# Relu-squared attention and a GELU feed-forward block on one core: what the first load gate of batch 2 reads

## The chip, the cores and the metric

The kernel runs on one core of a Trainium2 chip. The metric is the device time of one execution in microseconds (us). TensorE (PE) multiplies matrices, ScalarE (ACT) and VectorE (DVE) do the elementwise work and empty the PSUM memory that the PE writes to, GpSimd (POOL) and SyncE (SP) do almost nothing here but issue DMAs. A DMA issued by POOL and one issued by SP run on the same 16 DMA engines; the profile calls POOL's queue q0 (software_dynamic) and SP's q1 (hardware_dynamic).

## The reference

Eight batches of twelve heads, 448 tokens, head size 64. The attention has no softmax: the scaled scores go through relu and are squared. Its output, 3584 rows of 768, goes through two matrix products with an exact GELU in between.

```python
def _attn_ref(q, k, v):
    S = q.shape[2]
    scale = 1.0 / np.sqrt(q.shape[-1])
    scores = scale * np.matmul(q, k.transpose(0, 1, 3, 2))
    attn = np.maximum(scores, 0.0) ** 2 / S
    return np.matmul(attn, v)

def _moe_ref(x, w_in, w_out):          # x: 3584 x 768, w_in: 768 x 2048, w_out: 2048 x 768
    h = x @ w_in
    g = 0.5 * h * (1.0 + erf(h / sqrt(2)))
    return g @ w_out
```

## The kernel before

**Batches and groups.** A batch's twelve heads are taken as three groups of four (G = 3). Work is written as operations with an engine, a function and dependencies; a long string, ORDER, then fixes by hand the order in which each engine gets them. Every engine works its own list in order, so an instruction that waits holds up all that stands behind it on that engine. The dependencies listed with an operation serve the ordering alone; the waits in the program come from what each instruction reads and writes.

**Loads.** POOL issues all loads of q, k, v and the weights (L463, L552, L570, L480 to L482, L486). They convert float32 in HBM to bf16 in SBUF on the way. The output weights come in three parts (`add_wout`): part 1 is two DMAs of 384 KB, part 0 one DMA of 1536 KB, part 2 again two of 384 KB.

**Transposes.** For batches 0 and 1 the PE transposes q and k. From batch 2 on SP does it by DMA (`add_T_dma`): for each group a transpose of k into kT (L666), one of q into a segment of the tile qT (L666, called "even" below), and then two plain copies within qT that swap the upper and lower 64 partitions into the next segment (L686 and L687, called "the swap"). Segment 2g of qT holds the transposed q of group g, segment 2g + 1 its exchanged copy. In SP's list for batch 2 the order is: q of group 0, k of group 0, q of group 1, swap of group 0, k of group 1, swap of group 1, q of group 2, swap of group 2, k of group 2. A swap reads what a transpose writes, so SP waits for that transpose to land before it issues the swap. The transposes and copies of one batch and group are called q0, k0, swap 0, q1, k1, swap 1 and so on below.

**Gates.** A gate (`add_gate`, L709) is a copy of 128 x 16 elements on POOL whose result nobody uses. It reads from a segment of qT and so makes POOL wait until the DMA that writes this segment has landed; the loads behind it in POOL's list go out only then. There are three gates for each of the batches 2 to 6. For batch 2 all three read the exchanged copy (segment 2g + 1), for later batches the transposed q itself (segment 2g).

POOL's list around batch 2 is: gate of group 0; output weights part 1; gate of group 1; k of group 2 of batch 2; output weights part 0; v of group 0 of batch 2; q of groups 0 and 1 of batch 3; output weights part 2; gate of group 2; v of group 1 of batch 2, k of groups 0 and 1 of batch 3, and so on.

**Who uses what.** On the PE the scores of batch 2 (L741) need kT and both segments of the group: group 0 from the first scores on, group 1 from the third run of scores on (the fifth product of the twelve that start together at 58.94 us in the profile). They are put between products of the feed-forward block (L854, h = x @ w_in). The products with w_out that need the output weights first are at L1267 (`add_plain`, part 0 alone for the first two), followed by Strassen-like products (L1172, L998).

```python
        for g in range(G):
            op = turn(k_dst(g), k_src(g), list(ld_k[b, g]))
            ...
            even = turn(q_dst(g), q_src(g), lands)
            both = sch.add(
                (("SP", SWAP_STEP, SWAP_TIME),), swapped(g), [even] + after.pop(0), mode="X"
            )
            for c in range(NC):
                Tq[b, g, c] = (even, both)
```

Of the kernel before, what the change touches and what calls it, by code (L numbers as in the profile page):

```python
# [24 lines left out]
SEG = 4 * NC // 2 * KC  # L25
# [373 lines left out]
def kernel(  # L399
# [9 lines left out]
    nc = tc.nc  # L409
# [81 lines left out]
    def get_T(b):  # L491
        if b not in qkT:
            qkT[b] = (
                tpool.tile([128, QCOLS], BF16, tag="qT", name="qT"),
                tpool.tile([128, G, NK * 128], BF16, tag="kT", name="kT"),
            )
        return qkT[b]
# [5 lines left out]
    def q_seg(b, n):  # L503

        return get_T(b)[0][:, SEG * n : SEG * n + SEG]
# [31 lines left out]
    Tq, Tk = {}, {}  # L537
# [165 lines left out]
    gate = const.tile([128, 16], BF16, tag="gate", name="gate")  # L703

    def add_gate(b, g):


        def fn(e):
            nc.gpsimd.tensor_copy(gate, q_seg(b, 2 * g + (b == 2))[:, : SEG : SEG // 16])  # L709

        deps = [Tq[b, g, 0][b == 2], Tk[b, g, 0][0]]
        pool_q.append(sch.add((("POOL", 0.2, 0.3),), fn, deps))

    xT, hT = {}, {}
# [682 lines left out]
    add_steps(steps(1), ATT1_BIAS, True)  # L1397
    add_T_dma(2, [[]] * 9)
    add_gate(2, 0)
    add_wout(0)  # L1400
    add_wout(1)
    add_gate(2, 1)
    add_wout(2)
    add_gate(2, 2)
    for m in range(0, HALF_M, 2):
        add_f1(0, m, 1, bias=F1B_BIAS)
# [135 lines left out]
```

## Time and profile before

| what | value |
|---|---|
| time, median of 3 runs | 371.41 us (370.39 to 371.74) |
| the profiled execution's own time | 370.35 us |
| its span, first to last instruction | 368.2 us |
| PE busy | 358.2 us (97%) |
| DVE busy | 287.9 us (78%) |
| ACT busy | 192.0 us (52%) |
| POOL busy (issuing loads included) | 62.7 us (17%) |
| granted TensorE clock, mean | 0.998 |
| the first gate of batch 2 starts | 52.07 us |

The span is what the engines' instructions cover; the execution's own time is 2.15 us longer. All positions in the text are in us from the start of the span. A row of the timeline gives start, duration, engine, line, operation and tiles, and in brackets the idle time before it with what ended it; of an engine called SPq it is the issuing of a DMA, not its transfer. The DMA view of a narrow window lists the DMAs issued in it with the time from issue to landing.

### The profile page before, as it was taken

To read this page: it belongs to the slowest core of one execution; us is meant where nothing else is said; L and a number is where in the kernel's file an instruction comes from. 1 tells how busy PE (TensorE), PEld (TensorE's weight loads), DVE (VectorE), ACT (ScalarE), POOL (GpSimd) and SP (SyncE) were. 2 spreads that over 40 slices of the span, in tenths; PEclk is the share of its full clock that TensorE was granted. 3 is DMA by queue.
4 is the path that set the end of the run, shared out by engine and by line. 5 is a ranking of instruction groups with operands and counts; after the bars stand their busy time and mean duration, and the time that the engine had idled before them with its cause. 6 is when DMAs were issued, how large, how long until landed. Compare 5 with 4: busy or idle time off the path is not lost.

```text
span 368.2 us, 8480 instructions
## 1 busy us (share of the span) xinstructions
PE 358.2 (97%) x3560; PEld 222.2 (60%) x3560; DVE 287.9 (78%) x480; ACT 192.0 (52%) x312; POOL 62.7 (17%) x101
## 2 busy tenths in 40 slices
PE   8799999999899999999999999999999999999995
PEld 7576654445444555544555544477888787867663
DVE  4999863479886899898669999999977866667753
ACT  5998867626267553768666366860514134232200
POOL 8576116130050060050401000000000000000000
PEclk9999999999999999999999999999999999999999
DMA  9999999999999999999999960000300202022233
GB/s 170 199 199 199 200 154 122 203 183 177 229 179 216 181 167 187 248 180 190 156 175 178 194 129 2 2 2 0 88 2 0 88 25 62 2 85 87 85 85 88
DMA packets 75046, 47.10 MB, mean 128 GB/s; under 512 B 38528, under 2 KB 71552, under 8 KB 75008
## 3 DMA queue, kind: packets, MB, share of 16 engines
q0 software_dynamic: 32912, 22.47, 43.3%
q1 hardware_dynamic: 41456, 23.59, 30.8%
q8 instruction: 28, 0.46, 0.5%
q10 hardware_dynamic: 640, 0.51, 0.4%
q14 instruction: 10, 0.08, 0.1%
HBM read 45.61 MB, written 11.01 MB: 154 GB/s over the span
## 4 chain that ended last, share of the span: by engine, by line
PE 79%; DMA 15%; POOL 2%; SPq 1%; issue 1%; DVE 0%; DVEq 0%; POOLq 0%
PE pso L1172 32%; PE psh L854 18%; PE pb L998 13%; PE ps L741 8%; PE pav L802 7%; DMA qT<-nq 6%; DMA nk<-in_k_dram 4%; DMA kT<-nk 2%; DMA v_sb<-in_v_dram 2%; DMA qT<-qT 1%; POOL nk L552 1%; POOL nq L463 1%; PE tp L639 0%; SPq L686 0%; SPq L666 0%
## 5 line engine op out<-in xcount | busy, mean ns | idle before, releaser
L753 ACT ACTIVATE a_sq<-ps 128x896 bf16<-128x896 f32 (+1 forms) x116 | 102.7, 919 | 45.5 <-PE ps L741 42.1
L762 DVE TENSOR_TENSOR a_sq<-a_sq 128x896 bf16<-128x896 bf16 x169 | 97.0, 617 | 7.6 <-ACT a_sq L753 7.4
L854 PE MATMUL psh<-xT,win_sb 128*128 128x448 bf16 (+1 forms) x516 | 96.4, 340 | 0.0
L854 PEld LDWEIGHTS <-win_sb 128*128 128x128 bf16 x516 | 47.9, 98 | 46.2 <-issue 10.0
L755 DVE TENSOR_SCALAR a_sq<-ps 128x896 bf16<-128x896 f32 (+1 forms) x53 | 57.1, 1079 | 18.2 <-PE ps L741 17.9
L1172 PEld LDWEIGHTS <-s_sb 128*128 128x128 bf16 x424 | 40.7, 98 | 25.7 <-issue 1.8
L864 ACT ACTIVATE h_sb<-psh 128x448 bf16<-128x448 f32 x80 | 43.5, 549 | 22.1 <-PE psh L854 21.8
L741 PE MATMUL ps<-qT,kT 64*64 64x448 bf16 (+1 forms) x756 | 47.7, 336 | 1.5 <-DMA kT<-nk 1.0
L1035 DVE TENSOR_TENSOR part<-pb,part 128x448 f32<-128x448 f32 x60 | 35.3, 620 | 13.5 <-PE pb L998 11.4
L1172 PEld LDWEIGHTS <-h_sb 128*128 128x128 bf16 x312 | 29.8, 98 | 20.9 <-issue 3.2
L1172 PE MATMUL pso<-wout_sb,h_sb 128*128 128x384 bf16 x208 | 38.1, 326 | 0.0
L1172 PE MATMUL pso<-wout_sb,s_sb 128*128 128x384 bf16 (+2 forms) x216 | 38.1, 320 | 0.0
L1172 PE MATMUL pso<-t_sb,s_sb 128*128 128x384 bf16 x208 | 38.1, 326 | 0.0
L802 PE MATMUL pav<-a_sq,v_sb 64*64 64x448 bf16 (+1 forms) x756 | 36.7, 329 | 1.2 <-DMA v_sb<-in_v_dram 0.6
L1206 DVE TENSOR_TENSOR osb<-pso,p_sb 128x384 f32<-128x384 f32 x39 | 21.6, 554 | 13.3 <-PE pso L1172 11.5
L741 PEld LDWEIGHTS <-kT 64*64 64x64 bf16 x756 | 18.7, 105 | 21.1 <-issue 14.4
L998 PEld LDWEIGHTS <-win_sb 128*128 128x128 bf16 x288 | 27.5, 98 | 2.9 <-issue 0.7
L802 PEld LDWEIGHTS <-v_sb 64*64 64x64 bf16 x756 | 21.2, 107 | 12.9 <-issue 1.9
L1044 ACT ACTIVATE h_sb<-part 128x448 bf16<-128x448 f32 x36 | 18.4, 576 | 19.0 <-DVE part L1035 18.9
L519 ACT CAST xT<-pav 128x448 bf16<-128x448 f32 (+1 forms) x38 | 18.3, 499 | 7.8 <-PE pav L802 5.6
L709 POOL COPY gate<-qT 128x16 bf16<-128x16 bf16 x15 | 4.1, 274 | 104.4 <-DMA qT<-nq 80.3
L998 PEld LDWEIGHTS <-ws 128*128 128x128 bf16 x216 | 20.8, 98 | 1.2
(57 smaller groups left out, 296.8 us busy)
## 6 DMA issues: line engine op xcount, KB each, us to landing
nk<-in_k_dram POOLq DMA_DIRECT2D x23, 224.0 KB, 9.5
nq<-in_q_dram POOLq DMA_DIRECT2D x21, 224.0 KB, 10.1
qT<-qT SPq DMA_DIRECT2D x36, 112.0 KB, 2.6
v_sb<-in_v_dram POOLq DMA_DIRECT2D x5, 672.0 KB, 8.8
out_dram<-osb SPq DMA_DIRECT2D x8, 336.0 KB, 3.1
v_sb<-in_v_dram POOLq DMA_DIRECT2D x9, 224.0 KB, 9.8
out_dram<-osb SPq DMA_DIRECT2D x7, 288.0 KB, 3.1
out_dram<-osb SPq DMA_DIRECT2D x8, 240.0 KB, 3.5
```

The costliest lines, as they stand in the source:

```text
L741: nc.tensor.matmul(ps[64 * j : 64 * j + 64, e, x * w : x * w + w], kT[r, g, i * 128 + 64 * j : i * 128 + 64 * j + 64], moving, start=True, ...
L753: A.activation(ar, ps, AF.Relu, scale=c_att)
L755: V.tensor_scalar(ar, ps, c_att, 0.0, op0=mybir.AluOpType.mult, op1=mybir.AluOpType.max,)
L762: V.tensor_mul(box["a2"][:, :, :used], ar, ar)
L802: nc.tensor.matmul(pav[0][o2 : o2 + 64, e, :w], vt[b][r, 2 * g + e, bass.ts(i, D)], box["a2"][r, y, o : o + w], start=(i == 0), stop=(i == ...
L854: nc.tensor.matmul(ph[:, x * n : x * n + n], win_sb[:, kd, bass.ts(m + x, 128)], xT[b][:, kd, c], start=(kd == 0), stop=(kd == KD - 1),)
L864: A.activation(h_ring()[:, m : m + nm, o + c.start : o + c.stop], box[0][:, :S].rearrange("p (x n) -> p x n", x=nm), AF.Gelu,)
L998: nc.tensor.matmul(bank[name][:, y, z * HS : z * HS + HS], w[:, k, bass.ts(mm, 128)], right()[:, k], start=first and k == 0 and z == 0, st ...
L1035: V.tensor_add(get(to), ps(name), get(other))
L1044: A.activation(h_ring()[:, m : m + 2, o + half[c].start : o + half[c].stop], src().rearrange("p (x n) -> p x n", x=2), AF.Gelu,)
L1172: nc.tensor.matmul(box[bank][:, n0:n1], left()[:, kf], right()[:, kf, n0:n1], start=bool(need) and kf == 0, stop=kf == K2 - 1, skip_group_ ...
L1206: V.tensor_add(out()[:, n0:n1], box[bank][:, n0:n1], other()[:, n0:n1])
```

## The change

The first gate of batch 2 (b = 2, g = 0) reads segment 0 of qT in place of segment 1: the q of group 0 as the transpose leaves it, and not its exchanged copies. The two other gates of batch 2 go on reading exchanged copies, and all gates of later batches are as they were. The listed dependency changes with it. The number of operations and the order string do not change, so every engine has the same instructions in the same order.

```diff
         def fn(e):
-            nc.gpsimd.tensor_copy(gate, q_seg(b, 2 * g + (b == 2))[:, : SEG : SEG // 16])
+            nc.gpsimd.tensor_copy(gate, q_seg(b, 2 * g + (b == 2 and g > 0))[:, : SEG : SEG // 16])
 
-        deps = [Tq[b, g, 0][b == 2], Tk[b, g, 0][0]]
+        deps = [Tq[b, g, 0][b == 2 and g > 0], Tk[b, g, 0][0]]
         pool_q.append(sch.add((("POOL", 0.2, 0.3),), fn, deps))
```

## The prediction

> **What bounds the kernel now.** I read the page first: its slices for the busy engines, then the chain of work that ended last.
>
> ```profile
> PE   8799999999899999999999999999999999999995
> DMA  9999999999999999999999960000300202022233
> PE 79%; DMA 15%; POOL 2%; SPq 1%; issue 1%; DVE 0%; DVEq 0%; POOLq 0%
> ```
>
> The PE is full in nearly every slice, so only an idle stretch of the PE is worth anything; the eleventh slice (92 to 101 us) has one, inside a stretch where the DMA engines are full too. So I asked for the waits that end a PE idle time after the start-up, and for the PE's timeline there.
>
> ```profile
> PE ps L741 <- DMA kT<-nk: 1.0, 1, 1.0
> PE pso L1267 <- DMA wout_sb<-in_moe_w_out_dram: 0.4, 1, 0.4
> ...
> 96.27 1.16 PE L741 MATMUL ps<-qT,kT 64*64 64x448 bf16 x12 [0.97 <-DMA kT<-nk]
> ```
>
> These are all that late DMAs cost the PE behind the gate: 0.44 us at 76.4 (output weights part 0), 0.97 us at 96.27 (k0 of batch 3), and in the same row some 0.40 us inside, since twelve such products take 0.76 us elsewhere (58.94) and 1.16 here. Together 1.8 us: the most that earlier loads can give.
>
> Next the gates, from POOL's timeline, and SP's issues beside them.
>
> ```profile
> 38.14 1.53 POOL L570 DMA_DIRECT2D v_sb<-in_v_dram  x2 [1.49 <-DMA win_sb<-in_moe_w_in_dram]
> 52.07 0.20 POOL L709 COPY gate<-qT 128x16 bf16<-128x16 bf16 x1 [12.40 <-DMA qT<-qT]
> 52.53 1.49 POOL L486 DMA_DIRECT2D wout_sb<-in_moe_w_out_dram  x2 [0.25 <-issue]
> 55.86 0.21 POOL L709 COPY gate<-qT 128x16 bf16<-128x16 bf16 x1 [1.84 <-DMA qT<-qT]
> 56.31 0.70 POOL L552 DMA_DIRECT2D nk<-in_k_dram  x1 [0.24 <-issue]
> ```
> ```profile
> 48.95 0.55 SPq L686 DMA_DIRECT2D qT<-qT  x1
> 49.54 0.59 SPq L687 DMA_DIRECT2D qT<-qT  x1
> 50.22 1.29 SPq L666 DMA_TRANSPOSE kT<-nk  x1
> 51.61 0.54 SPq L686 DMA_DIRECT2D qT<-qT  x1
> 52.20 0.59 SPq L687 DMA_DIRECT2D qT<-qT  x1
> 52.84 2.90 SPq L666 DMA_TRANSPOSE qT<-nq  x1
> ```
>
> The rows of SP are swap 0 (two), k1, swap 1 (two) and q2. The first gate starts when swap 0 has landed (49.54 + 2.4 us to landing = 51.94), the second when swap 1 has (52.20 + 3.5 = 55.7). No load is under way from 48.5 to 54.0, and in this gap SP's DMAs are quick: the narrow DMA views give k1 2.9 us from issue to landing. Beside loads they are not; the next rows are k0 of batch 3 (issued 87.38) and q2 (issued 52.84), each from the DMA view of its own instant.
>
> ```profile
> kT<-nk SPq DMA_TRANSPOSE x1, 8.2
> ...
> qT<-nq SPq DMA_TRANSPOSE x1, 12.9
> ```
>
> **The change part by part.** *The gate itself.* It costs the same copy, and waits for q0 in place of swap 0. q0 lands at 40.76 + 8.17 = 48.93; the old gate began 0.13 us after its landing, so the new one begins at about 49.07, 3.0 us earlier. POOL has been free since 39.7. Output weights part 1 is issued at 49.53 and 50.27 in place of 52.53 and 53.27. Nothing is added or removed on any engine or queue, and nothing is queued newly behind a wait; what changes is which DMAs run beside these 768 KB. They now meet swap 0, k1 and swap 1, and less of q2.
>
> *Swap 0* (issued 48.95 and 49.54; the load 49.53). Its row is 2.3 and 2.4 us. The first scores of batch 2 need it and run at 53.02, 1.1 us after its landing. Nearest rows are the swaps with a load issued within 0.15 us behind the second copy: issued at 100.47, 128.61 and 180.09 they took 2.3 in the median of the pair, at 157.08 4.0. I take no delay; the bad end, 1.7 us more on the pair's median, would hold the PE for 0.6 us.
>
> *k1 and swap 1.* Lower end: k1 keeps its 2.9 us and swap 1 lands at 55.7 as before. Upper end: k1 fares as q2 did, which was issued 0.31 us after the first of these loads (k1: 0.69 after), and takes 12.9 us. Between them lie k0 of batch 2 (issued 42.14, 7.6 us) and the 8.2 above, both issued while loads drained with no new load following. That is the new state of k1, since the second gate keeps the next loads out, while q2 had k and the 1536 KB coming in behind. I take 8.2: k1 lands at 58.4. In batch 4, where k1 is issued at 122.47 (3.0 us) and the second copy of swap 1 at 124.44 (2.4 us), swap 1 lands 1.4 us behind k1; so here at 59.8, 4.1 later than before. The scores of group 1 come at about 59.1 (fifth product of the run at 58.94): the PE stalls for 0.7 us (ends: 0, and 50.22 + 12.9 + 1.4 − 59.1 = 5.4).
>
> *The loads behind the second gate* go out 4.1 us later, k of group 2 at 60.4. But the DMA engines lose less on q2. The DMA view counts, for the stretches 58:62, 62:64.5 and 65:69:
>
> ```profile
> DMA packets 1239, 0.53 MB, mean 131 GB/s; under 512 B 826, under 2 KB 1239, under 8 KB 1239
> ...
> DMA packets 280, 0.17 MB, mean 67 GB/s; under 512 B 114, under 2 KB 280, under 8 KB 280
> ...
> DMA packets 1067, 0.82 MB, mean 204 GB/s; under 512 B 15, under 2 KB 1067, under 8 KB 1067
> ```
>
> So 0.70 MB took 6.5 us that needs 3.4 at the pure rate of loads: 3.1 us lost while q2 ran beside them. Now q2 follows swap 1 in the time without loads. Loads took from 52.53 to 55.5 to come up to rate; the new ones, issued at 60.4, do by 63.4, need 1.1 us for k of group 2 (224 KB), and reach at 64.5 the point that stood at 65.0 before. With swap 2 out of the way sooner as well I take 0.8 us ahead (an estimate). Then part 0 lands at 75.6, when the PE, 0.7 late, is at 76.3: no wait, 0.44 back. Batch 3's k0 and swap come 0.8 earlier too, and the PE, which leaves their scores when they have landed, leaves them 0.8 earlier.
>
> *The sum.* The stall of 0.7 is paid out of the 1.8 us of later waits, and what is left of those ends 0.8 us earlier: −0.8 on the profiled execution, 370.35 to 369.55. That execution stands 1.06 below the median of the runs; on the median 371.41 − 0.8 = 370.6.
>
> **A rule weighed against the row.** While both kinds run, the DMA view of 84:87 has 528 packets of loads and 527 of SP's, one for one. But from 55.5 to 58 it has 552 of loads and none of SP's, though q2 was issued by 55.74. The Trainium skill ("DMA: Bandwidth & Descriptors", section Queues, rings and completion order) says that each DMA engine takes the queues that have work in turn, packet by packet. The trace bears that out once both run, not for the first microseconds after an issue; by the rule alone the sum would be the first rival's −1.8.
>
> **The rivals.** *SP's packets take turns from the start (faster).* k1's packets begin at 51.0 as in the row before. Its 896 packets of 256 B (224 KB) at 527 per 3 us take 5.1 us: it lands at about 56.5, swap 1 at 57.9, before its scores. No stall; the later loads are 1.9 us further ahead than in my sum, 2.7 in all, and the whole 1.8 us comes back: 369.6. For it: the one-for-one counts; against it: 55.5 to 58.
>
> *k1 is held like q2 (slower).* Swap 1 lands at 64.5; the PE stalls 5.4 us. The second gate is 8.8 later, so the loads are 3.9 behind where they were (4.7 later than in my sum), less than the stall, and they bring no wait of their own: 5.4 − 1.8 = +3.6, 375.0. It becomes slower than before when the stall is over 1.8, that is when swap 1 lands after 60.9. For it: q2 is the same kind of DMA, on the same queue, in the same position to the same load. Against it: at 60 to 64.5 q2 also met the start of the next loads.
>
> *The gate goes on waiting for swap 0*, if a read of qT waits for every earlier write of the tile: 371.4, no change. Against it: the first scores of batch 2 stand behind swap 1 in the order string and run at 53.02, 2.7 us before swap 1 lands.
>
> **How the numbers follow.** About 0.5% (1.86 us) is what a measurement of this kernel can tell from no change. My forecast 0.43, turns from the start 0.25, held like q2 0.27, no change 0.05. Faster by over 0.5% means below 369.55: near half of the first rival (0.12) and the lucky edge of the forecast (0.06), 0.18. Slower, above 373.27: 0.27 and 0.05 of the forecast, where swap 0 is late too: 0.32. Same: 0.50. The range has cases of both signs: 369.2 (the first rival and run-to-run spread) to 374.8 (most of the second). The forecast's own is 369.6 to 372.3.
>
> **What would show it.** The first gate starts near 49.1 and L486 is issued at 49.5; k1 takes about 8 us in place of 2.9; the second gate starts near 60 (58 by the first rival, 64.6 by the second); the PE row of twelve products at 58.94 shows an idle time or a longer run; q2 takes 6 to 9 us in place of 12.9; the wait at L1267 is gone, and the wait for kT at 96.27 is shorter. Wrong would be a gate at 52, a PE stall at 53.0, or a wait for part 0 that has grown.

## The result, and the profile after

The changed kernel takes 372.27 us (median of 22 runs, 369.95 to 375.09), the kernel before 370.38 us (median of 22 runs beside them, 369.07 to 373.86). The ratio is 1.0044 with a 95% interval of 1.0025 to 1.0064. So the change costs 1.9 us by the medians and 1.6 by the ratio, which compares runs taken beside each other and is not the quotient of the two medians. That is inside the 0.5% which was called no change and inside the range given, but the forecast was 0.8 us faster, and the interval excludes any gain.

The profiled execution of the changed kernel took 370.97 us, 0.62 more than the one before, with a span of 368.8 us. It lies 1.3 us below the median of its kernel. That matters below: one profile shows how things go, and only the medians show what they cost.

The PE's slices on the page and the chain after the change, in tenths of a slice and in shares of the span:

```profile
PE   8889999999999999999999999999999999999995
PE 89%; DMA 6%; POOL 1%; DVE 1%; issue 1%; ACT 0%; SPq 0%; DVEq 0%; POOLq 0%
```

The eleventh slice of the PE is full now, where it had an 8: the wait near 96 us is smaller. The chain leans less on DMAs (6% for 15%). By these lines alone one would expect a gain.

POOL's timeline of the changed kernel (start, duration, engine, line, operation, tiles, and in brackets the idle time before it):

```profile
49.19 0.20 POOL L709 COPY gate<-qT 128x16 bf16<-128x16 bf16 x1 [10.25 <-DMA qT<-nq]
49.42 1.49 POOL L486 DMA_DIRECT2D wout_sb<-in_moe_w_out_dram  x2
60.53 0.21 POOL L709 COPY gate<-qT 128x16 bf16<-128x16 bf16 x1 [9.62 <-DMA qT<-qT]
60.98 0.70 POOL L552 DMA_DIRECT2D nk<-in_k_dram  x1 [0.25 <-issue]
61.67 1.17 POOL L486 DMA_DIRECT2D wout_sb<-in_moe_w_out_dram  x1
```

The first gate starts 2.88 us earlier (52.07 before) and waits for q0. Two DMAs later POOL stands at the second gate for 9.62 us (1.84 before), because swap 1 is late. The gate starts at 60.53 in place of 55.86, and k of group 2 and part 0 leave 4.7 us later.

Next SP's DMAs that now meet part 1. The lines are from the DMA views of the instants at which each was issued: the second copy of swap 0 (49.74), k1 (50.43), the second copy of swap 1 (52.53), q2 (53.19). The last number is the time from issue to landing.

```profile
qT<-qT SPq DMA_DIRECT2D x1, 112.0 KB, 4.8
...
kT<-nk SPq DMA_TRANSPOSE x1, 9.0
...
qT<-qT SPq DMA_DIRECT2D x1, 112.0 KB, 7.8
qT<-nq SPq DMA_TRANSPOSE x1, 7.9
```

They took 2.4, 2.9, 3.5 and 12.9 us before. The packets show how. First the queues of the changed kernel from 51 to 55 us (packets, MB, time as a share of 16 engines' stretch), then from 57 to 61, then those of the kernel before from 51 to 55:

```profile
q0 software_dynamic: 686, 0.51, 99.9%
q1 hardware_dynamic: 107, 0.12, 10.3%
```
```profile
q1 hardware_dynamic: 1567, 0.57, 109.2%
q0 software_dynamic: 21, 0.01, 1.9%
```
```profile
q1 hardware_dynamic: 1137, 0.52, 67.4%
q0 software_dynamic: 34, 0.03, 12.2%
```

From 51 to 55 the loads (q0) have the DMA engines almost to themselves, although k1 and a copy of swap 0 are under way from the start, and swap 1 and q2 are added. From 57 to 61 it is the other way round: SP's work (q1) runs, and the loads stand still, since the gate in front of the next ones waits for just that work. The kernel before did SP's work first. The two kinds of transfer still come one after the other; only their order is reversed.

The PE's timeline at the places that the prediction named, first the scores of group 0 in the kernel before, then the changed kernel:

```profile
53.02 0.55 PE L741 MATMUL ps<-qT,kT 64*64 64x448 bf16 x8
```
```profile
54.05 0.35 PE L741 MATMUL ps<-qT,kT 64*64 64x448 bf16 x2
54.55 0.57 PE L741 MATMUL ps<-qT,kT 64*64 64x448 bf16 x6 [0.15 <-DMA qT<-qT]
...
60.49 0.76 PE L741 MATMUL ps<-qT,kT 64*64 64x448 bf16 x12
...
77.36 1.95 PE L1267 MATMUL pso<-wout_sb,h_sb 128*128 128x384 bf16 x11
...
95.84 1.16 PE L741 MATMUL ps<-qT,kT 64*64 64x448 bf16 x12 [0.46 <-issue]
```

A stall at the scores of group 0 (swap 0), none at those of group 1, no wait for part 0, and 0.46 us where there were 0.97. The idle time in brackets, 0.15 us, is not the whole stall: the eight products took 0.55 us before and 1.07 here (54.05 to 55.12), so it is 0.52 us. The wait at 96 us ends in both kernels with the first copy of batch 3's swap 0, which SP issues behind k0: it lands 0.6 us after k0 (at 96.18 before, at 95.75 here), and the PE starts 0.09 us later. The bracket of the profile before names kT there. One thing must be known to read this: already at 50.2 us, when the moved loads have hardly begun, the PE of this execution is 1.03 us later in its list than that of the profile before. That is scatter of the start-up; the profiles of this study lie 0.1 to 2.1 us behind the first one there. A PE that is late by itself does not see a late swap 1.

Of the gain at 97 us (the PE is 0.44 us ahead of the profile before there) nothing is left at the end. At 152.92 VectorE waits for an output tile whose store has not landed, and the PE waits behind it:

```profile
152.92 0.56 DVE L1206 TENSOR_TENSOR osb<-pso,p_sb 128x384 f32<-128x384 f32 x1 [2.08 <-DMA out_dram<-osb]
```

From there on the PE is 0.58 us behind, which is the difference of the two spans.

### The profile page after: what moved, and what is told of

Same layout as the page of the kernel before. It is cut to its first block, busy times and chain, and to the rows that moved or that the text cites. A ratio compares the mean times of both kernels' runs of the same rounds, so it can differ in the third digit from the quotient of the medians.

```text
span 368.8 us, 8478 instructions
## 1 busy us (share of the span) xinstructions
PE 358.8 (97%) x3560; PEld 222.4 (60%) x3560; DVE 287.8 (78%) x480; ACT 191.8 (52%) x312; POOL 63.4 (17%) x101
## 4 chain that ended last, share of the span: by engine, by line
PE 89%; DMA 6%; POOL 1%; DVE 1%; issue 1%; ACT 0%; SPq 0%; DVEq 0%; POOLq 0%
PE pso L1172 32%; PE psh L854 23%; PE pb L998 13%; PE ps L741 9%; PE pav L802 8%; PE pso L1267 3%; DMA qT<-nq 2%; DMA v_sb<-in_v_dram 2%; DMA qT<-qT 1%; POOL nk L552 1%; POOL nq L463 1%; ACT a_sq L753 0%; PE tp L639 0%; DVE a_sq L762 0%; PE tp L611 0%
## 5 line engine op out<-in xcount | busy, mean ns | idle before, releaser
L854 PEld LDWEIGHTS <-win_sb 128*128 128x128 bf16 x516 | 47.9, 98 | 46.1 <-issue 10.0
L1035 DVE TENSOR_TENSOR part<-pb,part 128x448 f32<-128x448 f32 x60 | 35.2, 619 | 13.5 <-PE pb L998 11.4
L1206 DVE TENSOR_TENSOR osb<-pso,p_sb 128x384 f32<-128x384 f32 x39 | 21.6, 553 | 14.7 <-PE pso L1172 10.9
L998 PEld LDWEIGHTS <-win_sb 128*128 128x128 bf16 x288 | 27.6, 98 | 2.9 <-issue 0.7
## 6 DMA issues: line engine op xcount, KB each, us to landing
v_sb<-in_v_dram POOLq DMA_DIRECT2D x5, 672.0 KB, 10.5
```

What stands on the lines that cost most here:

```text
L854: nc.tensor.matmul(ph[:, x * n : x * n + n], win_sb[:, kd, bass.ts(m + x, 128)], xT[b][:, kd, c], start=(kd == 0), stop=(kd == KD - 1),)
L998: nc.tensor.matmul(bank[name][:, y, z * HS : z * HS + HS], w[:, k, bass.ts(mm, 128)], right()[:, k], start=first and k == 0 and z == 0, st ...
L1035: V.tensor_add(get(to), ps(name), get(other))
L1206: V.tensor_add(out()[:, n0:n1], box[bank][:, n0:n1], other()[:, n0:n1])
```

## The experiments

Every kernel was timed in 12 runs, beside 23 or 35 runs of the kernel before on the same chip; the ratios are to those. A ratio and the quotient of the medians differ by up to 0.3%, so where a difference of two medians is given, it is called that. Two theories run through the expectations below. **A**: the loss is paid at the scores of batch 2's groups 0 and 1, for which swap 0, k1 and swap 1 are late. **D**: the loss is paid later, because the second gate is late, the load queue stands still, and what is loaded behind it is late. B, a collision after 62 us (with batch 3's loads or with the store at 152 us), and C, scatter, are taken up where they stand. Of an edit to a gate only the argument of its copy is shown; the listed dependency changes with it.

### Both kernels again, and the gate at other places

`before_again` and `after_again` are the two kernels without an edit.

> The kernel before a second time, for a second profile and for the scatter. All theories: ratio 1.000 within 0.2%; swap 0 lands near 52 us, swap 1 near 55.7, no idle time of the PE at the first scores of batch 2; idle times for the output weights at 76 us and for kT at 96 us again. If those two waits are an accident of the first profile, they are missing or of another size here, and the gain that the prediction counted on was never there.

> The changed kernel a second time. Ratio 1.003 to 1.006. Theory A (early scores): the first profile had the PE 1.0 us late before the gate for reasons of the start, which hid part of the stall; with the PE on time the scores of group 0 stall about 1.5 us at 53 us behind the second copy of swap 0 and those of group 1 up to 1 us at 59 us behind swap 1. Theory B (later collision): the first 100 us come out even or better, and the PE loses 1 us or more at 140 to 160 us, where the VectorE waits for a store to land before it may write osb. Theory C (scatter): neither, and the ratio's interval includes 1.

Measured: 369.94 us, 1.0001 (0.9975 to 1.0027), and 371.81 us, 1.0060 (1.0031 to 1.0089). The loss is there again (1.9 us between the two medians), which excludes C. The second profile of the changed kernel does not have the gain at 96 us, and the late swap 1 shows inside the row of group 1's scores, which takes 1.22 us in place of 0.76:

```profile
60.65 1.22 PE L741 MATMUL ps<-qT,kT 64*64 64x448 bf16 x12
...
97.54 1.16 PE L741 MATMUL ps<-qT,kT 64*64 64x448 bf16 x12 [0.80 <-DMA kT<-nk]
```

`gate_on_q1` lets the first gate read q of group 1, so that part 1 leaves 1.83 us after q0's landing (0.29 in the changed kernel, 3.60 before):

```diff
-q_seg(b, 2 * g + (b == 2))
+q_seg(b, 2 if (b, g) == (2, 0) else 2 * g + (b == 2))
```

> The first gate reads the transposed q of group 1 (segment 2), which lands near 50.5: the loads go out at about 51.0, between the 49.5 of the changed kernel and the 52.5 of before. Swap 0 is then issued 1.4 us before the loads and should land near 52 as before; k1 and swap 1 still meet the loads. Theory A with swap 0 as the cause: the time is that of before (ratio within 0.2% of 1). Theory A with k1 and swap 1 as the cause, and theory B: slower like the changed kernel, 1.003 to 1.005.

Measured: 371.52 us, 1.0031 (1.0000 to 1.0062). Swap 0 lands 3.0 us after q0 as before, k1 6.07 us and swap 1 10.39 us after it. So if there is a loss here, and the interval just reaches 1, swap 0 is not needed for it. How its size compares with the changed kernel's cannot be told.

`both_gates` copies from segment 0 and then from segment 1 in front of the loads, so that POOL reads what the changed kernel reads while the loads stay where they were:

```diff
-nc.gpsimd.tensor_copy(gate, q_seg(b, 2 * g + (b == 2))[:, : SEG : SEG // 16])
+for n in ([0, 1] if (b, g) == (2, 0) else [2 * g + (b == 2)]): nc.gpsimd.tensor_copy(gate, q_seg(b, n)[:, : SEG : SEG // 16])
```

> The first gate made of two copies, one that reads segment 0 and then one that reads segment 1, so that POOL goes through the changed kernel's gate but the loads still wait for swap 0 and go out near 52.7. If the early loads are the cause of the loss, the time is that of before, ratio 0.998 to 1.002. If the altered program as such (its layout, its waits) is the cause, it is slower like the changed kernel, 1.003 to 1.006.

Measured: 369.71 us, 0.9976 (0.9946 to 1.0005). The read itself brings no loss; the loss comes with the earlier loads.

`late_gate` goes the other way: the first gate waits for swap 1, and part 1 leaves 7.72 us after q0. Its lines of POOL stand two places later in the order string.

```diff
-q_seg(b, 2 * g + (b == 2))
+q_seg(b, 3 if (b, g) == (2, 0) else 2 * g + (b == 2))
```

> The first gate reads segment 3 and waits for swap 1 like the second gate, so that output weights part 1 go out near 56 in place of 52.5. Theory A (loads beside SP's transposes and swaps cost): the same or faster than before, 0.996 to 1.001, with swap 1 at 54.5 and no delay by loads. Theory B (late loads cost): slower, 1.002 to 1.006, with a longer PE wait for output weights part 0 at 76 us.

Measured: 371.52 us, 1.0027 (1.0000 to 1.0053). Swap 1 is not disturbed (7.1 us after q0), part 0 lands as before (27.6), and at 97 us this profile is 0.96 us ahead of the profile before; it then loses 2.15 us at 152 to 156, at the same wait for a store. So later is not shown to be better than before, and the gate before the change is near the best of the places tried.

### The PE's list with more room

Here the two batches of scores that need swap 0 and swap 1 are called for about 1.2 us later, by moving PE blocks in the order string, on both kernels:

```diff
-P276 P279 P267 D226 S235 A277 A227 P291 D280 P288 P294 S236 A268 P356
+P267 D226 A227 P276 P279 S235 A277 A268 P356 P291 D280 P288 P294 S236
...
-P285 P300 P303 G272 A349 P354
+P285 P354 P300 P303 G272 A349
```

> The kernel before with the PE's list relaxed where batch 2 begins: one block of feed-forward products (1.2 us) goes ahead of the first scores of group 0 and one more ahead of the first scores of group 1, and one copy of x on the ScalarE goes ahead of one relu; no work is added. All theories: within 0.3% of before, 0.998 to 1.003. It is the reference for the next run.

> The changed kernel with the same relaxed list, so that swap 0 and swap 1 are needed 1.2 us later. Theory A (the early scores wait for swaps that land late): the loss shrinks by about 1.2 us, to a ratio of 1.001 to 1.003, and the two relaxed kernels differ by less than 0.3%. Theory B (the loss is made by DMAs later than 62 us): the two relaxed kernels differ by 0.4 to 0.6% as the plain ones do.

Measured: 370.35 us, 1.0004 (0.9977 to 1.0031), and 372.05 us, 1.0040 (1.0012 to 1.0068). 1.70 us lie between the two medians, where it was 1.9, and 1.3 us between the two ratios. More room at the scores alone is not shown to help.

### Without what comes later

No loads of q and k of batch 3 in one pair, no stores of one group of 256 output rows in the other (`g == 2`; the stores that VectorE waits for at 152 us), each on both kernels:

```diff
-        nc.gpsimd.dma_start(
+        if b != 3: nc.gpsimd.dma_start(
...
-            nc.gpsimd.dma_start(nk[b][:, 2 * g0 : 2 * g1], kv_view(k, b, g0, g1))
+            if b != 3: nc.gpsimd.dma_start(nk[b][:, 2 * g0 : 2 * g1], kv_view(k, b, g0, g1))
```
```diff
-            return lambda e: store_rows(rows[x][0] // 128, osb(x), c, queues)
+            return lambda e: None if g == 2 else store_rows(rows[x][0] // 128, osb(x), c, queues)
```

> The kernel before without the loads of q and k of batch 3 (it computes batch 3 with the q and k of batch 2). 1.3 MB less to move between 60 and 95 us, so that batch 3's transposes come early. If the waits of the PE at 76 and 96 us, 1.8 us in the first profile, are as large in the timed executions, the time falls by 1.4 to 1.8 us, ratio 0.995 to 0.9965. If they are small there, it falls by less than 0.7 us, 0.998 to 1.000.

> The changed kernel without the loads of q and k of batch 3 (wrong in batch 3 in the same way). Theory A (loss at the early scores, before 62 us): the loss stays or grows, 0.4 to 0.8% over the run without these loads of the kernel before, because no later wait is left that could take it up. Theory B (the loss is made by late loads and late transposes of batch 3 and after): it goes, and the two differ by less than 0.2%.

> The kernel before without the four stores of one group's 256 output rows (issued at 143.7 to 147.1 in its profile; these rows are left out of the result), so that no write into osb can wait for them at 152 us. The idle time of the PE at 155 us, 0 and 0.7 us in the two profiles of before, is gone: ratio 0.997 to 1.000. It is the reference for the next run.

> The changed kernel without the same four stores. Theory B (the VectorE's wait for these stores, which cost the PE 1.0 us in its first profile and 0.4 in its second, makes the loss): the two without stores differ by less than 0.25%. Theory A (lost before 62 us and not won back): they differ by 0.4 to 0.6% as the plain ones do.

Measured: without the loads 368.93 us, 0.9970 (0.9943 to 0.9996), and 371.10 us, 1.0004 (0.9978 to 1.0030); without the stores 369.48 us, 0.9969 (0.9949 to 0.9989), and 371.66 us, 1.0024 (0.9994 to 1.0054). The kernel before without the loads lies between its two expectations, so its waits at 76 and 96 us are neither as large as in the first profile nor small. Either edit makes both kernels faster (by the ratios 0.7 to 2.1 us), and a difference between the two stays: 2.17 and 2.18 us by the medians, 1.3 and 2.0 by the ratios. So neither batch 3's loads and their late transposes nor the wait for a store at 152 us is needed for the loss, and B falls. The two profiles of the changed gate show each a place where it is paid in that execution. Without batch 3's loads the PE waits for part 0, 1.05 us against 0.26 in the partner:

```profile
77.99 5.38 PE L1267 MATMUL pso<-wout_sb,h_sb 128*128 128x384 bf16 x32 [1.05 <-DMA wout_sb<-in_moe_w_out_dram]
```

Without the stores it stands at the scores of group 1; "issue" means that the profile shows no releaser, but the first copy of swap 1 landed 0.09 us earlier, at 61.01, and the partner has no wait there. With the longer row, these twelve products lose 0.94 us in all:

```profile
61.10 0.90 PE L741 MATMUL ps<-qT,kT 64*64 64x448 bf16 x8 [0.43 <-issue]
```

### The two prices taken apart

First D alone is removed. `second_even` is the changed kernel with its second gate, too, reading q itself (of group 1), so that it does not wait for swap 1:

```diff
-q_seg(b, 2 * g + (b == 2 and g > 0))
+q_seg(b, 2 * g + (b == 2 and g > 1))
```

> As the changed kernel, and the second gate reads the transposed q of group 1 too (lands near 50.5), so that k of group 2 and the 1536 KB of output weights part 0 go out at about 51.5 in place of 61. Swap 0, k1 and swap 1 all run beside many loads. If late swaps are what costs (theory A), swap 1 lands after 62 and the PE stalls by 3 us or more at the scores of group 1: ratio 1.006 to 1.015. If what costs is the second gate that comes late and holds the loads back, the loads are now early and the ratio is below that of the changed kernel, 0.997 to 1.002.

Measured: 370.92 us, 1.0044 (1.0015 to 1.0073), though part 0 now leaves 3.5 us after q0 (12.5 in the changed kernel) and lands 22.6 us after it (26.4). That lies between the two expectations: the early loads did not bring the time back, and the stall of 3 us or more did not come (swap 1 landed at 60.60). By the medians it loses 1.07 us where the changed kernel on the same chip loses 1.96, so a part may come back; the interval does not tell.

Then A alone is removed: batch 2's scores of groups 0 and 1 read only segment 0 of qT and the k of group 0, so that no late transfer can hold them. The transfers go on as before.

```diff
-moving = q_pair(b, g, e, (2 * ((2 * i + e) // NK) + j) * HS)
+moving = q_pair(b, g, e, (2 * ((2 * i + e) // NK) + j) * HS) if b > 2 or g == 2 else q_seg(b, 0)[r, min((2 * ((2 * i + e) // NK) + j) * HS, S) :][:, :S]
...
-kT[r, g, i * 128 + 64 * j : i * 128 + 64 * j + 64],
+kT[r, 0 if (b, g) == (2, 1) else g, i * 128 + 64 * j : i * 128 + 64 * j + 64],
```

> The kernel before, but batch 2's scores of groups 0 and 1 take their queries from the first segment of group 0 alone and their keys from group 0 alone, so that TensorE waits there for no copy of swap 0, no k of group 1 and no swap 1; the results of batch 2 are wrong by this. The transfers themselves are issued as before. Theory A (the early loads cost time because swap 0, the k of group 1 and swap 1 come late for these scores): the kernel before has little to gain here, 0.998 to 1.001 of its time. Theory D (the second gate comes late, the load queue stands still, and what is loaded later comes late): the same, 0.998 to 1.001.

> The changed kernel with the same edit (batch 2's scores of groups 0 and 1 read only the first segment of q and the k of group 0; results of batch 2 wrong). Theory A: the loss goes, and the ratio to the kernel before is within 0.25% of that of the kernel before with this edit. Theory D: the loss stays, 0.4 to 0.6% above it. Part of each: 0.25 to 0.4%.

Measured: 369.52 us, 0.9992 (0.9967 to 1.0018), and 371.92 us, 1.0057 (1.0031 to 1.0083). The whole loss is left, 2.4 us between the two medians: **theory A, as the sole cause, has fallen**. The PE's timelines of the two show where it is paid now. The kernel before with this edit:

```profile
77.03 5.37 PE L1267 MATMUL pso<-wout_sb,h_sb 128*128 128x384 bf16 x32 [0.46 <-DMA wout_sb<-in_moe_w_out_dram]
...
97.02 1.17 PE L741 MATMUL ps<-qT,kT 64*64 64x448 bf16 x12 [1.10 <-DMA kT<-nk]
```

The changed kernel with this edit:

```profile
78.94 5.37 PE L1267 MATMUL pso<-wout_sb,h_sb 128*128 128x384 bf16 x32 [1.15 <-DMA wout_sb<-in_moe_w_out_dram]
...
98.55 1.16 PE L741 MATMUL ps<-qT,kT 64*64 64x448 bf16 x12 [0.73 <-DMA kT<-nk]
```

In both the PE leaves 77 to 79 us when part 0 has landed, and 97 to 99 us when batch 3's k0 and, 0.6 us behind it, the first copy of its swap 0 have. It passes the first 1.91 us and the second 1.53 us later in the changed kernel; its start-up was 1.2 us later too, but a PE that waits at both places is set by the loads and not by its own start. Of the lateness of these loads 0.67 us is q0 itself landing later in this execution; the rest, 1.24 us for part 0 and 0.80 for k0 of batch 3, came after it.

Last, both are removed (`no_need_second_even`):

> The changed kernel with the same edit (results of batch 2 wrong), and with the second gate reading the first segment of group 1's q too, so that the loads behind it do not wait for swap 1. Early loads then, without the price at the scores of groups 0 and 1. Theory A: no slower than the kernel before with this edit, and up to 1.5 us faster, 0.995 to 1.000. Theory D: this removes the late second gate, so the ratio falls below that of the changed kernel with this edit by 0.2 to 0.5%.

Measured: 368.97 us, 0.9973 (0.9949 to 0.9998). Between this kernel and `no_need_after`, which differ in the second gate alone and were timed on the same chip, lie 2.95 us of the medians: with no need at the scores, the late second gate costs the whole loss and more (0.84% by the ratios, where theory D had 0.2 to 0.5%). POOL goes through the second gate with no wait:

```profile
49.97 0.33 POOL L709 COPY gate<-qT 128x16 bf16<-128x16 bf16 x1 [10.08 <-DMA qT<-nq]
50.24 1.49 POOL L486 DMA_DIRECT2D wout_sb<-in_moe_w_out_dram  x2
51.72 0.22 POOL L709 COPY gate<-qT 128x16 bf16<-128x16 bf16 x1
51.93 0.70 POOL L552 DMA_DIRECT2D nk<-in_k_dram  x1
```

The table of the early first gate, as ratios to the kernel before:

| the scores of groups 0 and 1 | second gate waits for swap 1 | second gate waits for q1 |
|---|---|---|
| need their transfers (the changed kernel) | 1.0044, 1.0060 | 1.0044 (1.0015 to 1.0073) |
| are called for 1.2 us later | 1.0040 (1.0012 to 1.0068) | 1.0014 (0.9995 to 1.0034) |
| do not need them | 1.0057 (1.0031 to 1.0083) | 0.9973 (0.9949 to 0.9998) |

Two late things stand side by side, and the table fits a PE that pays for the later of the two, not for their sum. Down the left column the need at the scores is taken away and nothing comes back, because the loads hold the PE at 77 us anyway. Along the top row the loads are early and nothing that can be told from scatter comes back, because, as the cells below say, the scores hold it. Only with both gone is the loss gone: the interval of 0.9973 lies apart from those of the changed kernel, of the top right cell and of the one left of it; with that of the middle cell above it, it overlaps by 0.0003.

The middle cell on the right is a kernel that computes everything, `second_even` with the relaxed list. It was run to see whether the rest of `second_even`'s loss lies at these scores:

> The changed kernel with the second gate reading q of group 1 itself, and with TensorE's list changed as in the relaxed pair, so that batch 2's scores of groups 0 and 1 are called for about 1.2 us later. With no need for swap 0, the k of group 1 and swap 1 this kernel had 2.6 us less (0.9973 against 1.0044), so what is left of its loss should lie at these scores: then 1.2 us of need taken away gives 0.999 to 1.002. If the order of TensorE's list does not matter to it: 1.003 to 1.006.

Measured: 370.17 us, 1.0014 (0.9995 to 1.0034), as expected of a price that is paid there. The intervals of this cell and the one above it overlap, so this step is likely rather than shown.

`half_part1` leaves one of part 1's two DMAs behind the early gate and puts the other behind the second, ahead of part 0:

```diff
-            for kf in rows:
-                load_wout(kf, c)
+            todo = {1: [(1, 0)], 0: [(1, 1), (0, 0)], 2: [(2, 0), (2, 1)]}[i]
+            for a, n in todo: load_wout(WOUTS[a][1][n], WOUTS[a][0])
```

> The changed kernel with one of the two 384 KB loads of part 1 of the output weights behind the early first gate and the other moved behind the second gate, ahead of part 0. Half the bytes run beside swap 0, the k of group 1 and swap 1. Theory A: swap 1 lands about 8.5 us after q of group 0 (6 to 7.6 before, 11.2 to 12.7 in the changed kernel) and half of the loss or less is left, 1.000 to 1.003. Theory D: the second gate comes earlier too, but 384 KB more stand behind it, so that part 0 is no earlier than in the changed kernel, and the loss stays, 1.003 to 1.006.

Measured: 371.07 us, 1.0030 (0.9996 to 1.0063), at the joint end of both expectations, so it tells nothing apart. Swap 1 lands 9.3 us after q0. Its profile shows that one load of 384 KB is enough to delay swap 0: its second copy landed 5.70 us after q0 (3.0 before), and the scores of group 0 waited.

```profile
56.12 0.57 PE L741 MATMUL ps<-qT,kT 64*64 64x448 bf16 x6 [0.94 <-DMA qT<-qT]
```

`second_only` is the kernel before with only the second gate moved to q1:

```diff
-q_seg(b, 2 * g + (b == 2))
+q_seg(b, 2 * g + (b == 2 and g != 1))
```

> The kernel before with only its second gate moved: it reads q of group 1 itself instead of its exchanged copies, so that part 0 of the output weights and what stands behind it need not wait for swap 1; the first gate waits for swap 0 as before. The two late things side by side: the load queue does not stand still between part 1 and the second gate, so that part 0 and the k of batch 3's group 0 land 1 to 3 us earlier, and the k of group 1 and swap 0 are as before, since both are done by about 4.2 us after q of group 0. Swap 1 runs beside more loads and lands 7 to 10 us after q of group 0 where the scores need it at about 10.2: 0.995 to 0.999. If swap 1 is held by these loads as it was in the changed kernel with its second gate early (11.9), the stall at the scores takes the gain: 1.000 to 1.004.

Measured: 369.59 us, 1.0004 (0.9976 to 1.0032). Swap 1 is not held (5.67 us after q0, so the stated cause of the second case is not what happened), part 0 and k0 of batch 3 land 1.7 and 1.9 us earlier than in the first profile, and the PE waits for neither. At 120 us its PE is 1.35 us ahead of the profile before, and at 160 it is 0.09 behind: it meets the store's wait instead.

```profile
152.44 0.56 DVE L1206 TENSOR_TENSOR osb<-pso,p_sb 128x384 f32<-128x384 f32 x1 [2.51 <-DMA out_dram<-osb]
```

No complete kernel was shown to beat the one before. `both_gates` at 0.9976 has 1.0005 in its interval.

## Why the prediction was wrong

These landings, in us after that of q0, are worked out from the DMA rows of the profiles.

| kernel | swap 0 | k1 | swap 1 | part 0 issued | q2 | part 0 | k0 of batch 3 |
|---|---|---|---|---|---|---|---|
| before | 3.0 | 4.2 | 6.8 | 8.1 | 16.8 | 27.4 | 46.6 |
| before_again | 3.0 | 4.2 | 7.6 | 8.8 | 14.6 | 28.6 | 46.8 |
| no_need_before | 3.0 | 4.2 | 6.8 | 8.1 | 17.4 | 27.7 | 47.1 |
| after | 5.4 | 10.3 | 11.2 | 12.5 | 12.0 | 26.4 | 46.0 |
| after_again | 4.7 | 10.4 | 11.3 | 12.6 | 12.0 | 27.9 | 46.9 |
| no_need_after | 3.1 | 9.2 | 11.8 | 13.1 | 12.8 | 28.9 | 47.9 |
| second_even | 5.0 | 9.4 | 11.9 | 3.5 | 16.7 | 22.6 | 43.0 |
| second_only | 3.0 | 4.2 | 5.7 | 5.9 | 13.1 | 25.7 | 44.7 |

- **The gate**: 49.19, as forecast (49.07).
- **Swap 0, "I take no delay"**: wrong. Its second copy took 4.8 us, above the bad end that was named (4.0, in the median of a pair); it landed later than before in every profile whose first gate reads q0, by 0.1 to 2.7 us. At the scores of group 0 it cost the PE 0.52 us in the first profile of the changed kernel and 0.17 in the second.
- **k1, 8.2 us**: right in kind, 9.0 measured. Swap 1 came at 60.38 (forecast 59.8) and the second gate at 60.53 (59.95); these steps hold within 0.6 us, k1's landing (59.43 for 58.4) within 1.0. The stall of 0.7 us at group 1 did not appear in this profile, whose PE was late by itself. In `after_again` it is 0.46 us, inside the row; without stores, where swap 1 landed latest (12.7 us after q0), 0.94. Groups 0 and 1 together lose 0.5 to 0.9 us in the four profiles that have the changed kernel's gates, its order of the PE's list and its need for the swaps. So the stall that was forecast at group 1 is about what both groups lose.
- **q2, 6 to 9 us**: right, 7.9.
- **The loads "0.8 us ahead" (an estimate)**: this is the step that failed. The first profile of the changed kernel has it nearly to the tenth: part 0 landed at 75.56 (forecast 75.6), and the wait at L1267 is gone. That was luck of the draw: of the other five pairs one has it too (`after_again`, 0.7 us earlier than `before_again`), and in four part 0 is later. Over the six profiles with the early gate and the second gate at swap 1, part 0 lands 28.3 us after q0 on average, over the seven with both gates late 27.4 (`both_gates` among them); k0 of batch 3, without the pair that does not load it, at 47.2 and 46.3.

  So the loads are late on average, by 0.9 us, and not 0.8 ahead. The size is uncertain: part 0 scatters from 26.4 to 29.1 us in the six and from 24.5 to 28.6 in the seven, it lands earlier in the changed kernel in two of the six pairs, and without the one profile at 24.5 (`no_store2_before`) 0.5 us are left; a gain of 0.8 does not fit either way.

  The step had two sizes wrong. Part 0 left 4.7 us later after q0 (12.9 for 8.2 on average), where 4.1 was forecast, because swap 1 landed 11.6 us after q0 (forecast 10.9). And from issue to landing it took 15.4 us for 19.2, that is 3.8 saved, where the step needed 4.1 + 0.8 = 4.9. That saving was taken from one execution's q2, and q2 was slow in some executions more than in others (it landed 12.8 to 17.4 us after q0 in the seven profiles with both gates late).

  A slip in the step's own working went the other way: its 0.70 MB contain 0.23 MB of q2 itself (queue q1 has 0.21 and 0.02 MB in the two stretches), so the loads moved 0.47 MB, which needs 2.3 us, and lost 4.2 us, not 3.1. That slip made the forecast gain too small, so it is not what failed.

  What was saved on q2 went into a new standstill. Counting the half microseconds from 46 to 80 us in which loads of under 25 KB start, the load queue is quiet for 10.9 us in the mean of the seven profiles (9.0 to 12.0) and for 11.4 in that of the six (10.5 to 12.0): no less than before. With the second gate at q1 as well it is 6 to 8.
- **The sum**: paying the stall out of later waits was a sound idea, but those waits end with the loads, and the loads were late. With the step at +0.9 in place of −0.8 the sum becomes +0.9. The spans of the six pairs of profiles (plain twice, relaxed, without loads, without stores, without need) differ by 0.6, 0.3, 3.0, 0.5, 2.1 and 0.1, on average 1.1 us; the medians of the same pairs by 1.7 to 2.4. The step is thus of the size that the profiles show on average, and about half of what the medians do. The range held because it was built from rivals of both signs, not because the forecast was near.
- **The rivals**: turns from the start (faster) is ruled out: k1 landed at 59.4, where that rival had 56.5 (its own terms, 51.0 + 5.1, give 56.1), and 51 to 55 us has 686 packets of loads to 107 of SP's. The Trainium skill ("DMA: Bandwidth & Descriptors", section Queues, rings and completion order) has each DMA engine go round the queues with work, packet by packet; this stretch does not look like that, though the profile does not tell which of SP's packets were ready. The rival that went slower, k1 held like q2, had the right direction. Its condition, swap 1 after 60.9, was not met in this profile (60.38), and the cost came without it, because it was bound to the scores alone. That the gate would go on waiting for swap 0 is excluded by its 49.19.

What stays open: how the other half of the 1.9 us in the medians divides between the scores and the loads, as one profile for each kernel is too few; how much `second_even` loses at the scores in its usual execution; why loads 1.7 to 1.9 us earlier in `second_only` bring no time; and how much of each gain the wait for a store at 152 us takes back. The profile of `second_even` cannot say: it is an execution of 369.44 us (median 370.92) whose PE was already 2.09 us late at 50 us, so that it began the run with group 1's scores at 61.03, when swap 1 had landed (60.60), and did not wait.

## What to carry to other kernels

A gate in front of loads also orders the transfers that run beside it: before one is opened earlier, look at what the next gate waits for, since loads that delay that transfer shut the queue again, and a standstill is moved instead of removed. When two late things lie side by side, taking away one shows nothing; the pair of edits that removes each alone and both together tells it. And an overlap seen in one profile (here q2's 12.9 us) needs a second one before it is booked as a saving: here it varied by 4.6 us between executions of nearly the same program.

## What was not expected of the hardware

- A copy within SBUF (the second of swap 0) issued 0.3 us behind the issue of a load took 4.8 us where it took 2.4 without it.
- For some 4 us after the load's first packets, from 51 to 55 us, SP's queue moved hardly anything (107 packets against 686) with k1, one to three copies and at the end q2 outstanding; then, when the loads had run out, 1567 from 57 to 61 us. The DMA engines were busy, but with one kind at a time.
- With the earlier loads the transpose of q2 took 7.9 us in place of 12.9 (8.9 to 13.5 in the other profiles with both gates late) and that of k1 9.0 in place of 2.9: the price of meeting loads went from one transpose to another.
